# Retention and MLP on one core: copies and v scaling given to other engines, one more tile transposed by DMA, a new order

## The chip, the core and the metric

The kernel runs on one core of one Trainium2 chip. The metric is device time in microseconds (us), the median of several runs. The engines are called as in the profile: PE is TensorE, DVE is VectorE, ACT is ScalarE, POOL is GpSimd, SP is SyncE (it only issues DMAs here).

## The reference

A retention recurrence with 4 batches, 8 heads, 768 positions and 64 channels a head gives `y`. An MLP with a residual is then applied to each position's 512 channels:

```python
gamma = 1.0 - 2.0 ** (-5.0 - np.arange(H))
for t in range(S):
    state = gamma * state + einsum('bhd,bhe->bhde', k[:, :, t], v[:, :, t])
    y[:, :, t] = scale * einsum('bhd,bhde->bhe', q[:, :, t], state)
x = y.transpose(0, 2, 1, 3).reshape(B, S, H * D)
xn = (x - mean) / sqrt(var + 1e-6) * g_ln
out = x + maximum(xn @ w_ch1, 0) @ w_ch2      # 512 -> 2048 -> 512
```

Inputs and output are fp32.

## The kernel before

**Tiles.** The positions are cut into chunks of 128, six a batch. That makes 24 tiles of 128 positions with all heads. Tiles 0 to 3 are the first chunks of the four batches; then come the five later chunks of each batch in turn (tile 4 is batch 0's second chunk, tile 9 is batch 1's).

**The order is written out by hand.** `ORDER` is one list of tokens. Each token emits the instructions of one small step, and each engine takes its own instructions in just that order; waits on data are added by the framework. A token has a name, a tile or group number, an optional engine after the first slash (A for ACT, D for DVE, S for SP) and, after the second, the PSUM banks that it writes. There are eight banks: X0 to X3, Y0, Y1, M and PD. `warm` tokens are matmuls on zeros that compute nothing.

**One tile, step by step.** The tokens and their lines:

- `k`, `q`, `v` (L340): loads from HBM, cast to bf16, issued by POOL. Tile 0's q and k come by `hk`, `hq` (L348, fp32, from ACT and SP) and are cast by `hkc`, `hqc` (ACT or DVE, L243, L245). `gk`, `gq`, `gv` (L369) are one-element copies on POOL that touch a buffer that is to be loaded anew.
- Tiles below `T0` have q and k transposed on PE (`tk`, `tq`, L375). `ek` (L245) copies k out of PSUM, and `eq` (L389) multiplies q by the decay table `qsc` on DVE. Later tiles have both transposed by one DMA on SP's queue (`tr`, L383), and `eq` then reads from SBUF and multiplies by the fp32 table `arg`.
- `vis` (L398): the 128 x 128 scores of each head, into two X banks a tile; for tiles from `T0` on also q times the state (L404). From tile 8 on, a visit takes two tiles at once.
- `am` (L411): scores times the decay mask, DVE. `py` (L426): scores times v, PE; for tiles 4 to `T0 - 1` also q times the state (L420).
- `vg` (L455): v times the decay table `vsc`, for the state. One POOL instruction of 128 x 512.
- `pd` (L463): k times that v, added up in bank PD over a batch's chunks. `pb` (L473) makes the bf16 state of the next chunk from it, on DVE. A batch has one state chain; three `vg` and three state buffers are in use in turn.
- `bn`, `xn` (L434, L444): statistics and centred input of the MLP, DVE. `xc` (L450): a bf16 copy of y for the residual, ACT.
- `tx` and `ex` (L484, L245): transposes of `xn` on PE and a DVE copy out of PSUM for tiles below `TX` = 8. Later tiles take a DMA transpose on SP's queue (L493).
- `m` (L518): first MLP product, four blocks of 128 hidden channels for one tile (or a group of two or four tiles) into an X bank. `r` (L529 on ACT, L531 on DVE): relu out of that bank into `h1`.
- `z` (L541): second MLP product, in quarters of four blocks. `ad` (L548): scale by 1/std and add the residual, DVE. `st` (L555): store, from ACT's queue.
- `W`, `Z` (L359, L364): the two weights in four pieces each, cast to bf16, from POOL's queue.
- `sq`, `rs`, `sqt`, `gch`, `qsc`, `vsc`, `mask`, `zero`, `consts`, `idn`, `cm`, `lmul`, `arg`: tables, constants and standard deviations.

All DMAs share 16 DMA engines. [...]

## Time and profile before

| | |
|---|---|
| median of 3 runs | 214.94 us (214.89 to 215.52) |
| the profiled execution's own time | 215.48 us |
| its span in the profile | 213.7 us |
| PE busy | 205.1 us, 96% (`warm`: 10.5 us) |
| DVE, ACT, POOL busy | 135.1, 71.8, 97.9 us |
| `m` (L518) and `z` (L541) on PE, as listed | 93.7 us; 62.7 + 21.8 us and smaller groups |
| `vg` on POOL | 20 of 1091 ns |
| `eq` on DVE | 17 of 835 ns from `tr`, 7 of 416 to 424 ns from PSUM |
| `tr` on SP's queue | 17, median 7.4 us to landing |
| store to landing | 2.7 us |

The span runs from the first to the last instruction of one execution; 1.8 us of that execution's time lie around it. Busy time on PE counts matmuls whose ends are modelled. An engine's idle time matters only where PE waits for it.

### The profile page before, as it was taken

The page shows a single profiled execution, that of the slowest core. Times are in us where ns is not written, and L with a number is a line of the kernel's source. Part 1 is how long each engine was busy: PE and PEld are TensorE (multiplying, and loading weights), DVE is VectorE, ACT ScalarE, POOL GpSimd, SP SyncE. Part 2 cuts the span into 40 slices and gives each one's busy share as a digit, 9 for nine tenths or more (in the row PEclk, how much of TensorE's full clock was granted, in tenths as well). Part 3 has the DMA queues.
Part 4 walks back from the last instruction along what each step waited for, and adds up shares of the span by engine and source line. Part 5 has one row for each costly group of instructions (what it writes and reads, how often), then busy time and mean ns, then how long its engine had stood idle before and what let it go on. Part 6 is the DMA issues. An engine that isn't in the chain of part 4 may idle for free.

```text
span 213.7 us, 4986 instructions
## 1 busy us (share of the span) xinstructions
PE 205.1 (96%) x2035; PEld 132.1 (62%) x2035; DVE 135.1 (63%) x309; ACT 71.8 (34%) x157; POOL 97.9 (46%) x145
## 2 busy tenths in 40 slices
PE   7989989999999999979999999999999999999994
PEld 2558889887566657647678678565545444444443
DVE  6798899858739878699469357598787401030023
ACT  5133635342211511603505523423092620444400
POOL 8986585892796880886775279210000000000000
PEclk9999999999999999999999999999999999999999
DMA  9999999999999999999999999966132230121005
GB/s 127 175 180 180 166 192 169 204 151 148 114 120 193 74 175 121 145 205 148 137 136 181 150 121 176 165 99 198 25 75 26 59 95 0 49 98 49 33 19 196
DMA packets 109946, 27.11 MB, mean 127 GB/s; under 512 B 102625, under 2 KB 106977, under 8 KB 109922
## 3 DMA queue, kind: packets, MB, share of 16 engines
q0 software_dynamic: 77024, 13.37, 89.1%
q1 hardware_dynamic: 28242, 6.85, 25.1%
q10 hardware_dynamic: 4656, 6.56, 9.5%
q8 instruction: 16, 0.26, 0.5%
q14 instruction: 8, 0.07, 0.1%
HBM read 27.30 MB, written 6.29 MB: 157 GB/s over the span
## 4 chain that ended last, share of the span: by engine, by line
PE 72%; DMA 16%; POOL 6%; DVE 3%; issue 1%; POOLq 0%; DVEq 0%; SPq 0%
PE X L518 29%; PE M L541 24%; PE Y L541 9%; DMA tr<-qk 5%; DMA q<-in_q_dram 4%; DMA v<-in_v_dram 4%; PE PD L541 3%; DMA qk<-in_q_dram 3%; PE X L398 2%; DVE trq L389 2%; PE Y L426 2%; PE PD L463 2%; POOL v L340 1%; POOL q L340 1%; POOL k L340 1%
## 5 line engine op out<-in xcount | busy, mean ns | idle before, releaser
L518 PE MATMUL X<-xnt,w 128*128 128x128 bf16 (+2 forms) x896 | 93.7, 257 | 0.9 <-DVE xnt L245 0.6
L529 ACT ACTIVATE h<-X 128x512 bf16<-128x512 f32 x88 | 50.5, 600 | 105.8 <-PE X L518 97.9
L518 PEld LDWEIGHTS <-w 128*128 128x128 bf16 x896 | 66.6, 98 | 22.2 <-issue 1.1
L541 PE MATMUL M<-w,h 128*128 128x512 bf16 (+1 forms) x272 | 62.7, 370 | 0.0
L541 PEld LDWEIGHTS <-h 128*128 128x128 bf16 x400 | 37.3, 98 | 37.6
L411 DVE TENSOR_TENSOR asb<-X,mask 128x512 bf16<-128x512 f32 x48 | 30.4, 683 | 7.9 <-PE X L398 7.7
L455 POOL TENSOR_TENSOR vg<-v,vsc 128x512 bf16<-128x512 bf16 x20 | 21.7, 1091 | 8.9 <-DMA v<-in_v_dram 6.7
L340 POOL DMA_DIRECT2D v<-in_v_dram x24 | 21.8, 909 | 3.6 <-DMA w<-in_moe_w_ch_dram 2.0
L434 DVE BATCH_NORM_STATS2 bns<-Y 128x6 f32<-128x256 f32 (+1 forms) x40 | 17.0, 461 | 9.6 <-PE Y L426 9.4
L541 PE MATMUL Y<-w,h 128*128 128x512 bf16 (+1 forms) x96 | 21.8, 370 | 0.0
L450 ACT CAST x_all<-Y 128x256 bf16<-128x256 f32 (+1 forms) x40 | 15.1, 417 | 16.7 <-DVE xn L444 14.3
L444 DVE SCALAR_TENSOR_TENSOR xn<-Y,mv,gb 128x256 bf16<-128x256 f32 (+1 forms) x40 | 19.1, 515 | 0.5
L473 DVE TENSOR_TENSOR state<-PD,gch 64x256 bf16<-64x256 f32 x40 | 16.7, 416 | 3.6 <-PE PD L463 3.2
L548 DVE SCALAR_TENSOR_TENSOR osb<-M,rstd,x_all 128x512 f32<-128x512 f32 (+1 forms) x17 | 12.2, 720 | 7.9 <-PE M L541 7.7
L340 POOL DMA_DIRECT2D qk<-in_q_dram x17 | 15.1, 888 | 1.3 <-issue 1.1
L340 POOL DMA_DIRECT2D qk<-in_k_dram x17 | 15.3, 898 | 0.5 <-issue 0.4
L548 DVE SCALAR_TENSOR_TENSOR osb<-PD,rstd,x_all 128x512 f32<-128x512 f32 x2 | 1.5, 752 | 21.5 <-PE PD L541 21.5
L389 DVE TENSOR_TENSOR trq<-tr,arg 128x512 bf16<-128x512 bf16 x17 | 13.9, 835 | 1.4 <-DMA tr<-qk 1.3
L548 DVE SCALAR_TENSOR_TENSOR osb<-Y,rstd,x_all 128x512 f32<-128x512 f32 (+1 forms) x6 | 4.3, 727 | 15.8 <-issue 11.4
L369 POOL COPY scrap<-qk 1x1 bf16<-1x1 bf16 x28 | 5.3, 188 | 17.3 <-DMA qk<-in_q_dram 9.0
L562 PE MATMUL PD<-zeros 128*128 128x512 bf16 (+1 forms) x37 | 9.5, 392 | 1.2 <-DVE zeros L249 1.2
L426 PEld LDWEIGHTS <-asb 128*128 128x128 bf16 x192 | 7.7, 98 | 2.1 <-DVE asb L411 0.7
(74 smaller groups left out, 133.3 us busy)
## 6 DMA issues: line engine op xcount, KB each, us to landing
out_dram<-osb ACTq DMA_DIRECT2D x23, 256.0 KB, 2.7
w<-in_moe_w_ch_dram POOLq DMA_DIRECT2D x8, 512.0 KB, 9.6
v<-in_v_dram POOLq DMA_DIRECT2D x24, 128.0 KB, 6.4
qk<-in_k_dram POOLq DMA_DIRECT2D x17, 128.0 KB, 6.8
qk<-in_q_dram POOLq DMA_DIRECT2D x17, 128.0 KB, 6.3
k<-in_k_dram POOLq DMA_DIRECT2D x6, 128.0 KB, 8.3
q<-in_q_dram POOLq DMA_DIRECT2D x6, 128.0 KB, 7.6
tr<-qk SPq DMA_TRANSPOSE x17, 7.4
```

Of the source, the lines that this page charges most:

```text
L340: nc.gpsimd.dma_start(out=dst, in_=tok[kind][TILES[t]])
L389: nc.vector.tensor_tensor(out=slot(trq, t), in0=x, in1=qsc if t < T0 else arg, op=ALU.mult)
L411: nc.vector.tensor_tensor(out=slot(asb, t)[:, :, par, :], in0=bank(("pa", t, par)).rearrange("p (i t) -> p i t", t=P), in1=mask.rearrange( ...
L434: nc.vector.bn_stats(out=bns[:, t, i, :], in_=x)
L444: nc.vector.scalar_tensor_tensor(out=dst, in0=src, scalar=mv[:, t, 0:1], in1=g, op0=ALU.subtract, op1=ALU.mult)
L450: nc.scalar.copy(out=dst, in_=src)
L455: nc.gpsimd.tensor_tensor(out=slot(vgs, chunk(t)), in0=v_of(t), in1=vsc[:, c, :].unsqueeze(2).to_broadcast([P, H, D]), op=ALU.mult)
L473: nc.vector.tensor_tensor(out=slot(state, chunk(t) - 1)[o, :, o], in0=pd[o, :, o], in1=gch[o, c - 1, :].unsqueeze(2).to_broadcast([D, NPAI ...
L518: nc.tensor.matmul(bank(("mm", g, ho))[:, j * n * P:(j + 1) * n * P], lhsT=w1[:, ko, (ho + j) * P:(ho + j + 1) * P], rhs=x[:, x0:x0 + n, k ...
L529: nc.scalar.activation(out=dst, in_=src, func=AF.Relu)
L541: nc.tensor.matmul(bank(("m2", t, piece))[:, 0:hi - lo], lhsT=slot(h1, t // 4)[:, ho, t % 4 * P:(t % 4 + 1) * P], rhs=w2[:, ho, lo:hi], st ...
L548: nc.vector.scalar_tensor_tensor(out=slot(osb, t + piece)[:, 0:hi - lo], in0=bank(("m2", t, piece))[:, 0:hi - lo], scalar=rstd[:, t:t + 1] ...
```

## The change

Six things are changed:

- `T0` goes from 7 to 6, so tile 6's q and k are transposed by DMA, and the `k0` buffers go from 7 to 6.
- `ek` and `ex` (below `TX`) carry their engine in the token. Four of the six `ek` and four of the eight `ex` are on ACT, the others on DVE.
- `vg` can run on ACT, as eight activations (`Copy` with a scale from `vsc`), one a head. The five of tiles 0, 4, 5, 6 and 7 stay on POOL; fifteen go to ACT.
- `qscf`, which made the fp32 table in `arg`, is gone; `eq` multiplies by the bf16 table `qsc` in all tiles.
- The order is a new one throughout. `gch` and `sqt` come early, the state memsets (`zero`) and `consts` later; `hkc0` comes before `vsc`; `vg0` comes right after W0.
- The `warm` matmuls are 20 wide and 17 narrow ones instead of 23 and 14.

```diff
-CFG = {'T0': 7,
+CFG = {'T0': 6,
...
-           'k0': 7,
+           'k0': 6,
...
-hk0b/A hk0a/S iota small pos hq0b/A hq0a/S v0 grow table zero touch k1 idn lmul q1 consts arg
-vsc v1 hkc0/A qsc hqc0a/D W0 warm8_0 tk0//Y0 cm hqc0b/A k2 ek0 warm2_3 tq0//Y1 eq0 q2 mask
...
+hk0b/A hk0a/S iota small pos hq0b/A hq0a/S v0 grow table idn cm touch k1 arg lmul q1 hkc0/A vsc
+v1 hqc0a/D W0 warm8_1 tk0//Y0 hqc0b/A ek0/D qsc consts zero warm1_2 tq0//Y0 gch eq0 sqt vg0/
+mask warm2_3 vis0//X1,X3 gb//X2 k2 tk1//Y1 tq1//Y0 q2 am0a am0b ek1/A gl eq1 W1 warm2_3 py0//Y0
...
-    @on("qscf")
-    def _(eng):
-        nc.scalar.activation(out=arg, in_=arg, func=AF.Exp, bias=ln8, scale=1.0)
...
-        nc.vector.tensor_tensor(out=slot(trq, t), in0=x, in1=qsc if t < T0 else arg, op=ALU.mult)
+        nc.vector.tensor_tensor(out=slot(trq, t), in0=x, in1=qsc, op=ALU.mult)
...
+        if eng == "A":
+            for h in range(H):
+                nc.scalar.activation(out=slot(vgs, chunk(t))[:, h, :], in_=v_of(t)[:, h, :],
+                                     func=AF.Copy, scale=vsc[:, c, h:h + 1])
+            return
```

Three stretches of the new order, around the steps that the prediction speaks of:

```
Z1 r3_12/D ex4/D rs1 py5//Y1 Z2 m2_12//X1 bn5 tr6 m4_0//X0 m4_8//X3 pb6 xn5 ...
pd6 r4_4/A m5_12//X0 eq6 vg7/ Z3 pb7 vg1/A k9 vis6//X3,X2 m5_4//X1 am6a am6b ...
r7_4/A z4_2 vg11/A rs4 eq11 eq10 z4_3 ad4 rs7 tr13 sq6 vis10//X1,X2,X3,X0 tr12 pd11 ...
```

## The prediction

> **What bounds the kernel now.** I read the summary and the slices first: is one engine full throughout?

> ```profile
> span 213.7 us, 4986 instructions
> PE 205.1 (96%) x2035; PEld 132.1 (62%) x2035; DVE 135.1 (63%) x309; ACT 71.8 (34%) x157; POOL 97.9 (46%) x145
> ...
> DMA  9999999999999999999999999966132230121005
> ```

> TensorE (PE) is busy 96%, but part of that is `warm` filler (L562, 10.5 us), and the DMA rings are full for two thirds of the span. So I asked where PE stands still, by stretches (columns: stretch; length; busy us and instructions of each engine; granted clock; DMA share; GB/s):

> ```profile
> 16.00:49.00 33.00, 31.15 (x553) 28.48 (x552) 27.43 (x58) 14.31 (x33) 23.88 (x27) 1.00 1.90 176
> 49.00:66.00 17.00, 16.77 (x192) 10.93 (x184) 11.00 (x24) 3.51 (x7) 12.20 (x21) 1.00 2.08 131
> 66.00:94.00 28.00, 26.62 (x300) 17.96 (x293) 22.88 (x49) 8.75 (x22) 18.30 (x31) 1.00 1.60 147
> 94.00:211.00 117.00, 116.77 (x908) 67.61 (x906) 61.40 (x135) 39.66 (x86) 28.98 (x46) 1.00 0.83 104
> ```

> Idle on PE: 1.85, 0.23, 1.38 and 0.23 us. That is 3.7 us after 16 us: all that a better order can win there. The chain of waits in order of time says what holds it (start, length, piece):

> ```profile
> 37.35 10.51 DMA tr<-qk
> ...
> 89.88 3.04 DVE trq L389 x2
> ...
> 93.06 0.62 PE X L398 x16
> ...
> 210.81 0.35 DVE osb L548
> ```

> Tile 7's DMA transpose took 10.51 us; two `eq` took 3.04 us ahead of `vis12`. From the groups and timelines come the durations (count, busy us, mean ns):

> ```profile
> L455 POOL TENSOR_TENSOR vg<-v,vsc 128x512 bf16<-128x512 bf16 x20 | 21.7, 1091 | 8.9 <-DMA v<-in_v_dram 6.7
> ...
> L389 DVE TENSOR_TENSOR trq<-tr,arg 128x512 bf16<-128x512 bf16 x17 | 13.9, 835 | 1.4 <-DMA tr<-qk 1.3
> ...
> L245 DVE COPY trk<-Y 128x512 bf16<-128x512 bf16 x7 | 2.9, 418 | 0.1
> ...
> L506 ACT ACTIVATE rstd<-mv,epsb 128x1 f32<-128x1 f32 x8 | 2.0, 287 | 0.1
> ...
> L389 DVE TENSOR_TENSOR trq<-M,qsc 128x512 bf16<-128x512 bf16 x4 | 1.7, 416 | 0.0
> ...
> L313 ACT ACTIVATE gch<-lgq 128x4 f32<-128x4 f32 x5 | 0.6, 206 | 0.0
> ```

> and ScalarE's timeline (start, length) shows the table load finished before k0 is there:

> ```profile
> 1.88 1.28 ACT L292 ACT_TABLE_LOAD   x1 [1.88 <-issue]
> ...
> 4.15 0.62 ACT L243 CAST k<-osb 128x512 bf16<-128x512 f32 x1 [0.47 <-DMA osb<-in_k_dram]
> ```

> **My yardstick** is the lag L: the time of a point in PE's order minus the useful PE work ahead of it. Prices from the chain's own pieces: `m` 0.875 us, a `z` quarter 0.863, `vis` 0.28 a tile (0.40 with its state part), `py` 0.235 (0.455 with state), `pd` or four transposes 0.22, `gb` 1.1. Added along the order this is 192.3 us before. Before: L is 11.9 at `m0_0` (16.28 us), 14.7 at 21.3 us of work (36.03), 15.6 at `pd6` (44.39), 15.7 at `vis7` (48.66), 16.3 at `vis8`, 16.7 at `vis10`, 18.1 at `vis12` (93.06), 18.5 at the end (210.8).

> [...]
> - [...] most `eq` on tr take 0.69 us, but the two at 89.88 took 1.5 each while two `vg` ran on GpSimd (89.88 to 92.37).
> - [...] The trace has 0.416 with the bf16 table (PSUM source) and 0.69 with the fp32 table; from SBUF with bf16 it shows none.
> - [...] `gch` 206, `sq` with a pointer 287.
> - [...] tr landed in 9.7 to 10.5 us beside loads, 3.0 when loads were over (147.7).

> **The change part by part.**
> *Fifteen `vg` from GpSimd to ScalarE.* Each becomes eight 128x64 activations with a pointer scale. [...] The next: two `sq` in a row took 0.47, so 0.18 for one column[...]. [...] ScalarE gains 30 us in all, 72 to about 106 of 214; not the bound on average. But it is in order: behind a `vg` wait the `r` (L529) that free PE's X banks, `xc`, and the stores; if v is late, all of them. Three places are tight by the order: `vg11` begins about 58.2 us of work (after `r7_4` and copies), ends 60.2, `pd11` stands at 59.4; `vg2` 73.9 against 73.3; `vg15` 86.2 against 85.4. In full 2.2 us of PE wait. ScalarE's starts there rest on three copies placed by the order, not by their data, so I take 0.9. At 1.3 us none waits.
> On GpSimd 15 × 1.09 = 16 us go; its loads can issue earlier [...]: the 3.04 us before `vis12` becomes about 0.8, and its 1.28 us of PE idle goes. Next late there is tr12/tr13 (landed by 87.7); needed at 89.0.
> *The bf16 table.* `qscf` (0.72, ScalarE) goes[...]. Hidden by matmuls except in the place just counted: 0.
> *Copies.* Nine of 0.42 us leave VectorE (one with tile 6, eight to ScalarE at about 0.5). ScalarE is idle 18.7 of the 33 us there; 0 beyond the walk below.
> *Tile 6.* On PE 0.44 us of transposes go, and the state part costs 0.12 instead of 0.22: useful work 191.7, so -0.5. Added: one 256 KB transpose on SP's queue, in front of tr7, and a wait of `eq6` on it; behind `eq6` on VectorE stand `pb7` and both `am6`.
> *The start.* In the compiled order the table load is ScalarE's first computing instruction and stands behind the landing of SP's half of k0 (3.74 us): 3.74 + 1.28 = 5.02, k0's cast to 5.7, `tk0` 0.9 late. The state memsets (0.82) now stand before `eq0`: 7.5 instead of 6.86. Then `eq1`, `bn0`, `xn0` come before `am1`: `tx0` 12.9 (13.19 before), `m0_0` 14.9, `m0_4` 17.1 with 5.3 us done: L 11.8, as before: 0. `vg0` stands behind W0 on GpSimd and waits for v0 (6.58): k2 to k3 issue 1.8 late, but the rings still hold W0; I take 0.4 us for all later loads.
> *17 to 35 us, walked with these prices.* Waits after: 0.85 at `tq3` (q3 landed 20.0, now 20.4), 0.35 at `m2_4`, 0.4 elsewhere (`z1_0` on Z0, now held back by `vg4` until v4 is there). `m2_12` at 35.0, 21.3 us done: L 13.7 against 14.7: -1.0.
> *35 to 50 us.* Loads before q6 are as many bytes as before less one v: q6 lands about 35.1. tr6 beside v6, v7, Z1, Z2: nearest rows 10.5, 10.1, 9.7, and 5.9 at less load; I take 9.5: 44.6, `eq6` to 45.05. PE reaches `vis6` (28.7 us of work) at 43.1: waits 2.0. L 16.4 against 15.6: a lag of 0.8, which the lead above is already in. Bounds: tr6 in 7.4 (median of all), no wait, a lead of 1.2; in 10.5, a lag of 1.8. tr7 lands 3 us after tr6, before `vis7` at 50.9: 0.
> *After `vis7`.* Before L grew 2.8; now 0.6 to `vis12`, 0.9 for `vg`, 0.4 to the end: 1.9, so -0.9. The closing 2.9 us (last add and store) are as before.

> Sum: +0.8 - 0.9 - 0.5 = **-0.6 us**. The profiled execution took 215.48 (span 213.7 and 1.8 around it); the median of the runs is 0.54 under it, 214.94. So 214.9 for such an execution, **214.3** for the median. About 0.3%, 0.64 us, is what a measurement can tell from no change.

> **The rivals.**
> - *Slower: `vg` holds up ScalarE.* Place: `pd11`, `pd2`, `pd15`. For it: eight short instructions where there was one, in order, before relus. Against: ScalarE is half idle. The waits in full at 2.0 are 2.2 (+1.3 on the sum: 215.6), at 2.7 they are 4.3 (217.7); middle 216.6. It decides from waits of 2.1 us, a `vg` of about 2 us.
> - *Faster: the stages close up.* tr6 lands within 7.4: -2.0, 212.3; with `vg` at 1.3 too: 211.4. For it: the median landing; against: the three loaded ones.
> - *No change:* a bf16 table that speeds up nothing costs nothing either, and the stall before `vis12` may be tr13's; then +0.6: 214.9.

> **How the numbers follow.** My case (213.7 to 214.9) has 0.40, half of it under 214.3; the faster rival 0.25, the slower 0.35. So faster 0.45, same 0.20, slower 0.35. Range 211.6 to 217.2: the faster rival's ends, and the slower one's middle and a little more. My own case's range is 213.7 to 214.9.

> **What would show it.** Table load near 3.8 and `tk0` near 5.7; eight L454 activations in about 2.0 us; `eq` under 0.45 and never 1.5; PE waiting for tr6 before `vis6` near 43; no idle before `vis12`. If PE idles near `pd11`, `pd2`, `pd15` or before X writes by more than 2 us, the slower rival holds; with no wait at `vis6`, the faster one.

## The result and the profile after

The change makes the kernel slower. Four runs of it took 221.91 to 226.08 us, median **224.29**; the kernel before, on the same chip, 215.23. The ratio is **1.038** (95% interval 1.033 to 1.044). Here and below, medians are of all runs of a kernel, and ratios leave out those more than 1.5% above its fastest, such as the run of 226.08. The profiled execution took 221.91, against 215.48 before: 6.4 of the 9.1 us can be followed in the traces. The other three runs have no trace.

The summary, the granted clock and the DMA row of the kernel after:

```profile
span 219.9 us, 5073 instructions
...
PE 205.2 (93%) x2009; PEld 133.7 (61%) x2031; DVE 125.0 (57%) x302; ACT 103.1 (47%) x285; POOL 80.4 (37%) x130
...
PEclk9999999976999999999999999999999999999999
DMA  9999999999999999999999999973002030302213
```

The work has moved as the edit says: ScalarE from 71.8 to 103.1 us, GpSimd from 97.9 to 80.4, VectorE from 135.1 to 125.0. PE is as busy as before, in a longer span. New is the clock row: two slices (44 to 55 us) in which the granted clock is not full. The same stretches as before (stretch; length; busy us and instructions of PE, PEld, DVE, ACT, POOL; clock; DMA share; GB/s):

```profile
16.00:49.00 33.00, 27.65 (x479) 25.51 (x480) 22.45 (x46) 15.71 (x36) 23.17 (x27) 0.96 1.74 164
49.00:66.00 17.00, 16.84 (x172) 12.26 (x174) 10.45 (x25) 6.19 (x17) 7.19 (x14) 0.88 1.76 142
66.00:94.00 28.00, 27.43 (x304) 18.79 (x306) 20.37 (x52) 15.75 (x50) 16.95 (x33) 1.00 1.82 158
94.00:217.00 123.00, 120.22 (x944) 69.69 (x954) 60.53 (x139) 58.55 (x169) 18.84 (x37) 1.00 0.77 101
```

Idle on PE is 5.35 us in the first stretch (1.85 before), 0.57 in the third (1.38 before), 2.8 in the last (0.23 before). The second is full, but at clock 0.88: 172 instructions where there were 192. The groups that answer to those shown of before (count, busy us, mean ns):

```profile
L454 ACT ACTIVATE vg<-v,vsc 128x64 bf16<-128x64 bf16 x120 | 30.0, 338 | 0.9 <-ACT h L531 0.7
...
L386 DVE TENSOR_TENSOR trq<-tr,qsc 128x512 bf16<-128x512 bf16 x18 | 7.3, 413 | 4.7 <-DMA tr<-qk 4.7
L395 PE MATMUL X<-trq,tr 64*128 64x128 bf16 x144 | 6.0, 222 | 3.7 <-DVE trq L386 3.7
```

`eq` from `tr` fell from 835 to 413 ns, and PE waited 3.7 us in one place for one of them. The chain, in order of time, says which and why:

```profile
18.18 8.57 DMA v<-in_v_dram
...
26.83 1.04 POOL vg L457
27.87 0.76 POOL w L361
28.63 0.90 POOL qk L337
29.52 0.98 POOL vg L457
30.51 6.38 DMA qk<-in_q_dram
...
36.97 9.61 DMA tr<-qk
...
46.60 0.44 DVE trq L386
...
47.17 0.61 PE X L395 x8
47.78 0.21 PE Y L401 x8
47.99 1.82 PE X L520 x16
```

Read it from the top. v4 is issued at 18.18 and lands at 26.8. `vg4`, which waits for it, stands on GpSimd's queue ahead of the load of k6, and `vg5` ahead of q6. So q6 is issued at 30.51, lands at 36.9, its transpose lands 9.6 us later, and `vis6` starts at 47.17. The kernel before has `vg4`, k6, `vg5` and q6 in the same order on this queue; its lines for v4, `vg4` and q6:

```profile
16.12 0.88 POOL L340 DMA_DIRECT2D v<-in_v_dram  x1 [0.75 <-DMA w<-in_moe_w_ch_dram]
...
25.84 1.04 POOL L455 TENSOR_TENSOR vg<-v,vsc 128x512 bf16<-128x512 bf16 x1 [0.98 <-DMA v<-in_v_dram]
...
29.32 0.94 POOL L340 DMA_DIRECT2D q<-in_q_dram  x1
```

There v4 was issued 2.1 us sooner and landed 1.0 us sooner, and q6 landed at 35.7. It did no harm, since tile 6 then needed no DMA transpose.

In the last line of the chain 16 matmuls take 1.82 us, for which 0.875 is the price: they run at half pace. One step finer, PE's clock beside its idle time:

```profile
40.00:45.00 5.00, 3.48 (x63) 3.30 (x60) 1.10 (x2) 3.91 (x14) 5.00 (x6) 1.00 1.26 182
45.00:50.00 5.00, 2.83 (x36) 2.77 (x37) 2.46 (x5) 0.15 (x1) 3.66 (x5) 0.63 1.50 108
50.00:55.00 5.00, 4.95 (x52) 4.35 (x51) 3.37 (x8) 1.56 (x5) 0.12 (x1) 0.68 2.05 163
55.00:60.00 5.00, 4.95 (x80) 3.91 (x79) 3.31 (x9) 1.01 (x2) 1.13 (x6) 1.00 1.85 161
```

PE is idle from 43.5 to 47.2 (3.69 us); the clock is 0.50 from 46.3 to 53.2 us. It fell 2.9 us after PE had become idle, and it was full again after 6.0 us of work. The last section says what these times follow.

With the lag L (time less useful PE work ahead, as in the prediction), both profiled executions side by side:

| at | before | after | step before | step after |
|---|---|---|---|---|
| `vis5` | 14.5 | 14.2 | | |
| `vis6` | 15.5 | 18.5 | 1.0 | **4.3** |
| `vis7` | 15.7 | 21.4 | 0.2 | **2.9** |
| `vis12` | 18.1 | 22.4 | 2.4 | 1.0 |
| end of PE's work | 18.5 | 24.9 | 0.4 | **2.5** |

So +3.3 at `vis6`, +2.7 behind it, -1.4 to `vis12`, +2.1 to the end, -0.3 ahead of all this: +6.4, less 0.6 us of useful work. That is the 5.8 us by which PE's last work ends later (the addition behind it starts at 216.65, against 210.81). Another 0.4 us of the span lies behind that.

### The profile page after: what moved, and what is told of

The parts are those of the page before. It is cut to its first block, busy times and chain, and to the rows that moved or that the text cites. A ratio compares the mean times of both kernels' runs of the same rounds, so it can differ in the third digit from the quotient of the medians.

```text
span 219.9 us, 5073 instructions
## 1 busy us (share of the span) xinstructions
PE 205.2 (93%) x2009; PEld 133.7 (61%) x2031; DVE 125.0 (57%) x302; ACT 103.1 (47%) x285; POOL 80.4 (37%) x130
## 4 chain that ended last, share of the span: by engine, by line
PE 64%; DMA 20%; ACT 7%; DVE 3%; POOL 3%; issue 1%; ACTq 0%; DVEq 0%; SPq 0%
PE X L520 28%; PE M L543 20%; PE Y L543 8%; DMA tr<-qk 4%; DMA v<-in_v_dram 4%; DMA w<-in_moe_w_ch_dram 4%; DMA out_dram<-osb 4%; ACT vg L454 3%; DMA qk<-in_q_dram 3%; PE PD L543 3%; PE Y L423 2%; PE X L395 2%; ACT h L531 1%; POOL vg L457 1%; PE PD L465 1%
## 5 line engine op out<-in xcount | busy, mean ns | idle before, releaser
L531 ACT ACTIVATE h<-X 128x512 bf16<-128x512 f32 x88 | 50.9, 602 | 75.5 <-PE X L520 73.7
L520 PEld LDWEIGHTS <-w 128*128 128x128 bf16 x896 | 68.2, 100 | 22.0 <-DMA w<-in_moe_w_ch_dram 0.8
L543 PE MATMUL M<-w,h 128*128 128x512 bf16 (+1 forms) x271 | 64.4, 370 | 2.3 <-issue 0.6
L550 DVE SCALAR_TENSOR_TENSOR osb<-M,rstd,x_all 128x512 f32<-128x512 f32 (+1 forms) x18 | 13.0, 723 | 35.3 <-PE M L543 32.8
L454 ACT ACTIVATE vg<-v,vsc 128x64 bf16<-128x64 bf16 x120 | 30.0, 338 | 0.9 <-ACT h L531 0.7
L431 DVE BATCH_NORM_STATS2 bns<-Y 128x6 f32<-128x256 f32 (+1 forms) x41 | 16.9, 450 | 10.9 <-PE Y L423 10.8
L447 ACT CAST x_all<-Y 128x256 bf16<-128x256 f32 (+1 forms) x41 | 15.1, 402 | 15.7 <-DVE xn L441 15.5
L543 PE MATMUL Y<-w,h 128*128 128x512 bf16 x78 | 19.0, 379 | 0.1
L475 DVE TENSOR_TENSOR state<-PD,gch 64x256 bf16<-64x256 f32 x40 | 16.7, 416 | 3.9 <-PE PD L465 3.6
L337 POOL DMA_DIRECT2D qk<-in_q_dram x18 | 16.1, 893 | 1.2 <-DMA v<-in_v_dram 0.6
L386 DVE TENSOR_TENSOR trq<-tr,qsc 128x512 bf16<-128x512 bf16 x18 | 7.3, 413 | 4.7 <-DMA tr<-qk 4.7
L395 PE MATMUL X<-trq,tr 64*128 64x128 bf16 x144 | 6.0, 222 | 3.7 <-DVE trq L386 3.7
L564 PE MATMUL PD<-zeros 128*128 128x512 bf16 (+1 forms) x36 | 8.1, 362 | 1.4 <-DVE zeros L250 1.2
L395 PEld LDWEIGHTS <-tr 64*128 64x128 bf16 x144 | 4.2, 96 | 7.6 <-DMA tr<-qk 3.8
```

Of the source, the lines that this page charges most:

```text
L337: nc.gpsimd.dma_start(out=dst, in_=tok[kind][TILES[t]])
L395: nc.tensor.matmul(bank(("pa", t, par))[:, i * P:(i + 1) * P], lhsT=kT(t)[o, i, :], rhs=slot(trq, t)[o, i, :], start=True, stop=True)
L431: nc.vector.bn_stats(out=bns[:, t, i, :], in_=x)
L447: nc.scalar.copy(out=dst, in_=src)
L454: nc.scalar.activation(out=slot(vgs, chunk(t))[:, h, :], in_=v_of(t)[:, h, :], func=AF.Copy, scale=vsc[:, c, h:h + 1])
L475: nc.vector.tensor_tensor(out=slot(state, chunk(t) - 1)[o, :, o], in0=pd[o, :, o], in1=gch[o, c - 1, :].unsqueeze(2).to_broadcast([D, NPAI ...
```

## The experiments

Theory A: tile 6's transpose by DMA comes too late, PE waits, and its clock is halved. Rival B: ScalarE, full of `vg`, is what costs. Ratios are to the kernel before on the same chip: median 214.54 for e1 to e4, 215.16 for e5 to e8, 215.06 for e9, e10, b1 and b2, 214.55 for e11, b3 and b4, 215.28 for e12. Kernels of different chips are compared by their distance to it; the changed kernel lies 9.1 us above.

### Is it the wait for tile 6?

**e2_pe6**: tile 6 goes back to PE, all else stays.

```diff
-CFG = {'T0': 6,
+CFG = {'T0': 7,
...
-bn5 tr6 m4_0//X0 ... r0_12/D pd6 r4_4/A
+bn5 m4_0//X0 ... r0_12/D tk6//Y0 tq6//Y1 ek6/A pd6 r4_4/A
```

> The changed kernel with tile 6's q and k transposed on PE again (T0 = 7, tk6 and tq6 ahead of pd6), all else in the new order. Theory A: no wait for tr6 and no drop of the clock, 3.7 + 2.9 less, 0.5 more PE work: about 218.2 us. Rival B: no change beyond +0.5: 224 to 225.

Measured: 217.79, ratio 1.016 (1.008 to 1.023). L is 16.2 at `vis6` and 16.6 at `vis7`. As A says: the distance to the kernel before is 3.3 us and no longer 9.1. B expected no gain.

**e4_q6first**: tile 6 stays on the DMA, but its loads no longer stand behind `vg4` and `vg5`.

```diff
-eq4 vg4/ pb4 ... r2_8/A Z0 am4a ... am4b k6 ex3/A ... vg5/ q6 py4//Y0 ... z1_0//M Z1
+eq4 k6 q6 vg4/ pb4 ... r2_8/A am4a ... am4b ex3/A ... vg5/ Z0 py4//Y0 ... Z1
...
-m5_12//X0 eq6
+m5_12//X0 z1_0//M eq6
```

> The changed kernel with k6 and q6 issued ahead of vg4 and of Z0 on GpSimd's queue, Z0 after vg5, and z1_0, which needs Z0, moved behind m5_12 on PE. Theory A: q6 lands about 33.4 us instead of 36.9, tr6 about 43, when PE gets to vis6: no idle, no drop of the clock, about 6 us less, 218.3. If tr6 is still 2 us late, the clock's drop is shorter or gone: 220 to 222. Rival B: no change.

Measured: 217.55, ratio 1.014 (1.008 to 1.020); no wait for tile 6 (L 16.4, then 16.9). The distance is 3.0 us: the same gain by another way. What PE still waits for in this kernel (us in total, times, longest):

```profile
PE M L542 <- DVE osb L549: 1.3, 1, 1.3
...
PE PD L464 <- POOL vg L456: 0.9, 1, 0.9
PE X L519 <- DMA w<-in_moe_w_ch_dram: 0.8, 1, 0.8
PE Y L371 <- ACT k L243: 0.7, 1, 0.7
```

**e3_vgpool**: all `vg` on GpSimd again, the rest as changed.

```diff
-vg1/A ... vg9/A ... vg10/A ...
+vg1/ ... vg9/ ... vg10/ ...
```

> The changed kernel with all vg on GpSimd, as one instruction each, at the same places of the order. Rival B: most of the loss goes, 3 to 6 us less, 218 to 221. Theory A: the wait before vis6 and the clock's drop are still there (vis6 near 47, vis7 near 55.6); at most the 1.2 us by which the lag grew more after vis7 than before the change go[...]: 222.5 to 225.5.

Measured: 221.87, ratio 1.028 (1.017 to 1.039), between the two forecasts. The distance is 7.3 us, only 1.7 less than the changed kernel's, so B is not the main cause; e2 and e4, which leave the `vg` on ScalarE, say so more firmly. A was wrong on the clock: PE came to `vis6` late in this trace (46.1, after a slow start, see below), waited only 2.0 us, and its clock was not halved. A `vg` on GpSimd held it up 1.35 us at 107 us.

**b4_tr6**: the old order, with tile 6 on the DMA and the bf16 table, and nothing else of the change.

```diff
-CFG = {'T0': 7,
+CFG = {'T0': 6,
...
-m4_12//X1 bn5 ... tq6//Y0 rs5 tk6//Y1 r4_0/A eq6 ... ek6
+m4_12//X1 tr6 bn5 ... rs5 r4_0/A eq6 ...
```

> The kernel of b2 (old order, bf16 table) with tile 6's q and k transposed by DMA instead of by TensorE: tr6 stands ahead of bn5 on SP's queue, as in the changed kernel, and the loads of k6 and q6 stay where the old order has them. Theory A (the transpose needs its lead, whatever the order): q6 is issued at about 28 us there, lands at 34, the transpose takes 9.6 us and the multiplication 0.4, so that vis6 can start at 44.5 at the earliest; TensorE, with 0.7 us less to do, is there at 39.6: it stands idle 4 to 5 us, its clock is halved for about 6 us (mean granted clock 0.982 to 0.986), and the time is 213.9 - 0.6 + 4.5 - 1 + 2.9 = 219.7 us (218 to 221). Rival: the old order leaves the transpose enough time (the queue of loads on GpSimd is shorter there): no idle time over 2 us, no halved clock, 213.5 to 215.5 us.

Measured: 224.28, ratio 1.046 (1.038 to 1.054), 9.7 us above the kernel before and worse than expected. Its chain:

```profile
29.02 6.81 DMA qk<-in_q_dram
...
35.91 12.09 DMA tr<-qk
...
48.02 0.43 DVE trq L388
```

The transpose took 12.1 us to land here, not 9.6, and PE stood idle 8.7 us. So the wait comes with the transpose, in either order; the new order even shortens it.

### Is it the halved clock too?

**e1_fill** (the changed kernel) and **e6_tablefill** (e5, below) have 16 matmuls of zeros, 128x512 into X3, ahead of `vis6`: they compute nothing and only keep PE busy.

```diff
-k9 vis6//X3,X2
+k9 fill16//X3 vis6//X3,X2
```

> The changed kernel with 16 zero matmuls of 128x512 (3.5 us) into bank X3 ahead of vis6, in the 3.7 us in which PE stood idle for tr6; they compute nothing. Theory A (PE stands idle for tile 6's transpose, and its clock is halved after it): vis6 still starts near 47 us, but the clock stays full, and the 2.9 us by which the lag grew from vis6 to vis7 go: about 221.4 us against 224.3. Rival B (the eight-fold vg on ScalarE is what costs): no change, 224.3. Rival C (the clock's drop hides in waits on loads anyway): no change.

> The kernel of e5 with the 16 filling matmuls of zeros ahead of vis6. Theory A (the clock): the wait of 3.7 us for tile 6's transpose stays, since the matmuls only fill it, but the clock is not halved after it, so that the lag from vis6 to vis7 grows by 0.5 and not by 2.9 us: 221.0 - 2.4 = 218.6 us, granted clock 1.00 from 44 to 60 us. Rival B (the slow stretch after vis6 comes from the DMA traffic or from operands that come late, not from the idle time): the stretch stays slow, and the fill adds up to 0.5 us: 221.0 to 221.5 us.

Measured: e1 224.76, ratio 1.047 (1.040 to 1.054); e6 221.20, ratio 1.029 (1.021 to 1.036). In both, the clock stayed at 1.00 around `vis6`, and the lag grew by 0.5 (e1) and 1.4 us (e6) from `vis6` to `vis7` instead of 2.9. Of the two, e6 is the test: its other work was done at 43.6, and the fill lasted to 47.3, when tile 6 was there. In e1 the wait would have been 1.5 us only. The kernel of e6, same view as above:

```profile
45.00:50.00 5.00, 4.64 (x63) 3.10 (x62) 2.69 (x6) 0.82 (x2) 4.09 (x5) 1.00 1.51 104
50.00:55.00 5.00, 4.44 (x63) 3.00 (x61) 3.63 (x9) 1.42 (x4) 0.00 (x0) 1.00 1.97 167
```

In the second stretch, behind the wait, 63 instructions ran at full clock, where the kernel after managed 52. The operands are the same and the DMA traffic nearly so (167 GB/s, against 163), so it is the idle time that halved the clock there. The totals missed. e1's profiled execution lost 3.5 us ahead of `vis2`, and its fill (45.9 to 49.4) then held `vis6` up. Later PE waited 2.5 us for a buffer that a late store held (the chain is shown below, under e8), with the clock halved for 3.4 us behind it: from `vis14` to `vis16` L grew 4.4 us, against 0.7 in the kernel after. e6 came out 3.2 us under the median of all of e5's runs, where 2.4 were expected of the fill; but e5's ratio, from two runs, is 1.032 (1.019 to 1.046), from which e6's 1.029 can't be told. Between the two profiled executions (221.14 and 220.83) no gain shows either, since e6's was 1.0 us later at `vis5` and tile 6 came 1.7 us later. So the fill keeps the clock up, and what that is worth in the whole time is not shown.

The mean granted clock of every run says it for executions without a trace as well:

| kernel | runs | PE idle ahead of `vis6` in the trace | mean granted clock of its runs |
|---|---|---|---|
| after, e5, e9 | 12 | 3.2 to 4.3 us | 0.982 to 0.985, one 0.968 |
| b4_tr6 | 4 | 8.7 us | 0.974 to 0.977 |
| e6 (with fill) | 4 | none, filled | 0.998 to 1.000 |
| e1 (with fill) | 4 | none, filled | 1.000 twice, 0.992 twice (the wait at 116 us in the traced one) |
| e2, e4 (no wait) | 8 | none | 0.999 to 1.000 |

A clock of 0.984 over 220 us is 3.5 us of clock lost. The trace shows 2.4 us of it as lag (2.9 from `vis6` to `vis7` instead of 0.5); 0.4 fell into the end of the idle time.

### Is it the start?

**e5_table**: the table load early again.

```diff
-lmul q1 hkc0/A vsc v1
+lmul q1 vsc hkc0/A v1
```

> The changed kernel with one thing moved: the exponential vsc stands again ahead of the cast of tile 0's k on ScalarE's queue, as in the kernel before, so that ScalarE's table load runs while the DMA is on its way. Theory C (the start): the 0.8 us that TensorE stands idle at 4.9 us, for a cast that stands behind the table load, costs more than itself, because in most executions the matmuls of the first 14 to 17 us then run at half pace. So: tk0 at about 4.8 us with no idle time over 0.3, 0.40 us for its successors, the broadcast of g 1.1 us long and not 2.07, vis2 at about 15.5 us; 221.0 us (the profiled execution of the changed kernel, 221.9, less 0.8), 3 us under the changed kernel's median of 224.3, and the runs within 1.5 us of each other. Rival: the slow first 14 us of three of the profiles have another cause (the first matmuls' number, the DMAs); then the gain is at most the 0.8 us, 223.5 us, with runs as far apart as before.

Measured: 224.45 median (220.83 to 227.12), ratio 1.032 (1.019 to 1.046), an interval that says little. PE's first steps of this kernel, and then those of e3, which has the late table load:

```profile
1.59 3.30 PE L563 MATMUL PD<-zeros 128*128 128x512 bf16 x8
4.69 0.63 PE L371 MATMUL Y<-idn,k 128*128 128x128 bf16 x4
```

```profile
5.69 0.61 PE L371 MATMUL Y<-idn,k 128*128 128x128 bf16 x4 [0.80 <-ACT k L243]
...
6.82 0.58 PE L371 MATMUL Y<-idn,q 128*128 128x128 bf16 x4
```

The idle 0.8 us is gone, but `vis2` came at 16.07 (16.24 in the kernel after), and neither median nor spread moved: theory C's forecast fell. What stays is an observation: of six profiled executions with the late table load, three (e1, e2, e3) ran their matmuls at half pace until 14 to 17 us and reached `vis2` 2.6 to 3.7 us late; of the seven with the early one, none did (e7's lost 1.1 us later, at a half clock from 10.9 to 14.3 us). The clock row is full in e1, e2 and e3 all the same, but only because it counts time without a record as full: their clock records begin at 16.8, 13.9 and 17.2 us, those of the other traces at 4.0 to 7.0. Right there the matmuls go from half to full pace (wide ones on zeros from 0.43 to 0.22 us apart). So the slow start looks like half clock as well, and the mean clock (1.000 in e2 and e3) does not show it.

**e9_again**: the changed kernel unaltered, for a second trace.

> The changed kernel once more, for a second profiled execution, because the first (221.9 us) was the fastest of its four and the others, up to 226, have no trace. Theory C (slow start in most executions): a profile of 224 us or more has vis2 at 18.5 to 20 us and not at 16.2, and from vis5 on the same steps. Theory E (longer landings): vis2 at about 16.2, but the transpose of tile 6 lands later, 12 us and not 9.6, and TensorE stands idle over 5 us ahead of vis6. In both the clock is halved for about 6 us after the idle time, and the mean granted clock of every run is 0.982 to 0.986.

Measured: 223.92 (222.12 to 230.33), ratio 1.039 (1.032 to 1.046), profiled at 222.12. It had no slow start (`vis2` at 16.08); the transpose took 9.8 us, PE stood idle 4.3 us, and the clock was 0.982. The profiled execution was again the fastest of its four, so neither theory on the slower runs was put to the test.

### What is left once the wait is gone?

**e7_tableq6** is e4 with e5's edit. **e8_stores** is e7 with two stores put earlier on ScalarE's queue:

```diff
-st2/A r8_14/A ... st5/A r9_8/A ... r9_2/A st3/A vis14//X1,X0,X2,X3 st4/A vg16/A
+st2/A st3/A r8_14/A ... st5/A st4/A r9_8/A ... r9_2/A vis14//X1,X0,X2,X3 vg16/A
```

> The kernel of e4 (k and q of tile 6 loaded ahead of vg4) with the early table load of e5. If the two costs add up: e4's median 217.55 less 0.8 us of idle time, and less again if e4's runs had the slow start in part: 216.5 us (215.8 to 217.0); no idle time ahead of vis6, clock 1.00 at 44 to 60 us, lag at vis6 about 15.6 and at vis8 about 16.3, as in the kernel before. Left over are then about 1.5 us, from the stores and the scalings on ScalarE's queue at 100 to 125 us. Rival: the early start is eaten by the next wait (the landing of W1 or of tile 2's k and q), then 217.5.

> The kernel of e7 with two stores (tiles 3 and 4) put on ScalarE's queue earlier, beside those of tiles 2 and 5, instead of behind the scalings of v of tiles 14 to 16. Theory D: the wait of tile 9's result for a buffer whose store was issued late (1.26 us of TensorE in e4 at 113 us) goes: e7 less 1.2 us, 215.3 us, lag at vis16 about 18.5. Rival: the buffer that is waited for is another's, or the relus that are behind become the wait; then it is e7's time within 0.4 us.

Measured: e7 218.10, ratio 1.010 (1.006 to 1.015); e8 217.19, ratio 1.009 (1.006 to 1.013). e7 is no better than e4: the rival's 217.5 is the nearer one. In e8's trace no wait for an `osb` buffer is left; it had cost 0.3 us in e7's, 1.3 in e4's. But by the ratios e8 is only 0.2 us under e7, as the rival said, and not the 1.2 of theory D. In the kernel after, this chain had built up at 107 to 117 us:

```profile
106.94 1.90 ACT vg L454 x8
...
109.59 0.43 ACT x_all L447 x2
110.02 6.08 DMA out_dram<-osb
...
116.19 0.76 DVE osb L550
...
117.00 1.02 PE M L543 x4
```

A store stands behind a `vg` and copies on ScalarE's queue and lands late; VectorE waits for its buffer, PE for VectorE: 0.5 us here, 1.0 to 2.5 us in the traces of e1, e2, e4, e5, e6 and e9.

**e11_v6first**: e8 with v6 loaded ahead of v7, and `vg21`, `vg22` on GpSimd.

```diff
-r3_0/A v7 vis5//X3,X1 ... xc4 v6 tx4//Y0
+r3_0/A v6 vis5//X3,X1 ... xc4 v7 tx4//Y0
```

> The kernel of e8 (new order, tile 6's loads and the table load early, two stores early) with v of tile 6 loaded ahead of v of tile 7, and v of tiles 21 and 22 scaled by GpSimd again. Theory: two waits go that e8's trace shows, 1.2 us at 42.6 us (the state's product of tile 6 waits for vg6, which waits for v6's landing) and 0.5 us at 148.3 us (h behind vg22 on ScalarE): 217.2 - 1.5 = 215.7 us. Rival: vis6 then waits for the transpose that the 1.2 us hid: only the 0.5 us, 216.7.

Measured: 218.77 (217.41 to 220.76), ratio 1.023 (1.012 to 1.033). Neither theory. The two waits went (`vis6` at 43.07, L 14.4), and tile 7's transpose took them back. Its chain:

```profile
31.46 7.09 DMA qk<-in_q_dram
...
38.56 11.54 DMA tr<-qk
...
50.47 0.49 DVE xn L440
...
51.01 0.40 PE Y L485 x4
```

`eq7` waits for that transpose and holds half of `xn6` up behind it on VectorE; PE stood idle 3.1 us there, at a clock that stayed full.

**e10_allpool**: e8 with e3's edit.

> The kernel of e8 with all scalings of v on GpSimd again (1.05 us each instead of 2.0 on ScalarE). Theory B1: ScalarE's relus and stores are no longer behind the scalings; the waits on h (0.5 us at about 150 us) and on vg (0.5 us) go, and GpSimd, which also gates k, q and v, brings some back (1.35 us at 107 us in the kernel of e3): 216.2 to 217.2 us, no more than 0.8 us from e8's 217.2. Rival: GpSimd becomes the bound for the gates of the middle (80 to 130 us): 218.5 us or more.

Measured: 219.90, ratio 1.021 (1.015 to 1.027): 2.7 us worse than e8, the rival. PE waited 4.6 us for `vg` in three places. In the new order GpSimd cannot take the `vg` back.

**e12_pe6fix**: e2 with the repairs of e5, e8 and e11 (its `vg21`, `vg22`).

> The kernel of e2 (new order, tile 6's q and k transposed by TensorE) with the repairs of e5, e8 and e11: table load early, stores of tiles 3 and 4 early, v of tiles 21 and 22 scaled by GpSimd. Theory F (the transpose of tile 6 by DMA is all that is wrong with the change): no wait over 1 us is left anywhere, clock 1.00, lag 11.3 at vis2, 15.7 at vis8, 17.5 at vis14 and vis22: 214.3 us (213.5 to 215). Rival (the new order and the scalings on ScalarE cost something by themselves, spread over waits of 0.3 to 0.5 us): 215.5 to 217 us.

Measured: 215.48, ratio **1.001** (0.999 to 1.004), just under the rival's range and over theory F's. L is 16.2 at `vis8`, 17.8 at `vis14`, 18.2 at `vis22`, and the clock row is full. So with tile 6 on PE and three small repairs the rest of the change costs nothing that can be measured, and brings nothing. The repairs together take the distance from e2's 3.3 us to 0.2; which of them does it is not separated.

### Each part alone, in the old order

**b1_vg_act**: the fifteen `vg` on ScalarE, by the eight activations of the change.

```diff
-vg1 ... vg9 ... vg10 ...
+vg1/A ... vg9/A ... vg10/A ...
```

> The kernel before, in its own order, with one part of the change alone: v is scaled for the states by ScalarE, eight multiplications by a column each, for the same 15 tiles. Theory B1 (from the traces of the changed kernel: 8 in 2.00 us, relus and stores behind them late by up to 2.5 us in the stretch 100 to 155 us): it costs 1 to 2 us, 215.7 to 217 us, with TensorE waiting for h behind vg or for osb behind a store. Rival: GpSimd's queue was what held up the gates and so the transposes, and relieving it of 15 scalings (1.1 us each) gains about as much as ScalarE's loss: within 0.6 us of the kernel before.

Measured: 217.80, ratio 1.012 (1.005 to 1.018): 2.7 us slower, more than expected. Three waits of PE carry the loss (in brackets the idle time and its releaser):

```profile
105.15 0.81 PE L545 MATMUL M<-w,h 128*128 128x512 bf16 x3 [1.44 <-DVE osb L552]
...
134.49 1.03 PE L522 MATMUL X<-xnt,w 128*128 128x256 bf16 x8 [1.31 <-ACT h L533]
...
140.06 0.62 PE L397 MATMUL X<-trq,tr 64*128 64x128 bf16 x16 [0.86 <-ACT h L533]
```

The 2.7 us are net. With no `vg` on GpSimd beside them, the two `eq` ahead of `vis12` took 1.29 us and not 3.03, and the stall there was gone: L at `vis12` is 16.3, against 18.1 before. In this trace PE gained 1.8 us by then and lost 4.5 afterwards.

**b2_bf16**: the bf16 table alone.

```diff
-pd0 qscf q4
+pd0 q4
...
-in1=qsc if t < T0 else arg
+in1=qsc
```

> The kernel before, in its own order, with another part of the change alone: VectorE multiplies the DMA-transposed q by the bf16 table, and the exponential of the f32 table is left out. Theory: the multiplication takes 0.41 and not 0.84 us, and the stall before vis12 (lag 16.3 at vis8 to 18.1 at vis12; 16.9 to 17.5 in the kernel of e8) shrinks to 0.6 us: 1.2 us less, 213.8 us. Rival: the stall is one of DMA landings (the transposes of tiles 12 and 13), for which the multiplication comes 0.4 us sooner only: 0.4 us less; or nothing, within 0.3.

Measured: **213.89**, ratio **0.9955** (0.993 to 0.998): as expected, and the one version that beats both kernels. VectorE at the place in question, in the kernel before and then in this one:

```profile
89.88 3.03 DVE L389 TENSOR_TENSOR trq<-tr,arg 128x512 bf16<-128x512 bf16 x2
```

```profile
89.51 1.01 DVE L388 TENSOR_TENSOR trq<-tr,qsc 128x512 bf16<-128x512 bf16 x2
```

L grows 0.3 us from `vis8` to `vis12`, not 1.8: the stall was the multiplication's, and not a landing's. b1 and b2 together say that it needed both, the fp32 table and a `vg` on GpSimd: in these traces either part of the change ends it alone, so the gain comes once.

**b3_copies**: b2 with the copies of k and x split between ScalarE and VectorE as in the change.

```diff
-ek1 ... ex1 ... ek3 ... ek4 ... ex3 ... ek5 ... ex6 ... ex7
+ek1/A ... ex1/A ... ek3/A ... ek4/A ... ex3/A ... ek5/A ... ex6/A ... ex7/A
```

> The kernel of b2 (old order, bf16 table) with the copies of the transposed k of tiles 1, 3, 4, 5 and x of tiles 1, 3, 6, 7 by ScalarE instead of VectorE, as the changed kernel has them. Theory (the prediction's own reading: they are beside other work): within 0.5 us of b2, 213.4 to 214.4 us. Rival: on ScalarE they stand behind relus, and the matmuls that read them start later: 214.5 to 216 us.

Measured: 214.69, ratio 0.9995 (0.997 to 1.002): above the theory's range and in the rival's. By the ratios that is 0.9 us over b2, just clear of the noise. The rival's way is not what the trace shows: the copies did bring PE forward (L 13.3 at `vis6`, against 14.8 in b2), but `vis7` then waited 1.9 us for tile 7's transpose, and the clock dropped to half for 3.4 us: by `vis8` the lead had become a lag (17.6, against 16.1 in b2). Of the 19 runs in its ratio, seven have a mean clock of 0.991 or 0.992 and average 215.5 us; the other twelve average 214.1.

## Why the prediction was wrong

Predicted were 214.3 us and -0.6; it came to 224.3. Step by step, on the profiled execution:

- **The start and the walk to `vis6`: right within 0.4 us.** Table load at 3.75, `tk0` at 5.72, `tx0` 12.99 (12.9), `m0_0` 14.99 (14.9). L at `vis5` is 14.2, 0.3 less than before, and PE was ready for `vis6` at 43.5 (43.1).
- **tr6's wait (2.0 us, L 16.4): the term that was mis-sized first.** The transpose was right, 9.6 us against 9.5. Wrong was q6's landing, 36.9 and not 35.1. I had it follow from bytes in the rings, "as many bytes as before less one v", and from 0.4 us for all later loads. The chain shows that q6 is issued when GpSimd's queue gets to it, behind `vg4`, which waits for v4; that held before the change too. In the new order `vg0` stands ahead of k2, and the loads from there on were issued 0.9 to 2.1 us later than before. v4 landed 1.0 us later, and q6 was issued 1.2 us later; a v less in the rings brought nothing to a load that was not yet issued. (In e9 q6 was issued as early as before, at 29.26, and landed at 36.4.) I had seen `vg4` hold back Z0 and `z1_0`, and not the loads behind it. PE idled 3.7 us, and L became 18.5: 2.1 us more. My bound of a transpose in 10.5 us reached to a lag of 1.8 over before; measured are 3.0. e4 takes just these loads out from behind the `vg`, and the wait is gone.
- **What follows the wait: a term that the sum did not have.** I priced an idle time at its length. From `vis6` to `vis7` L grew 2.9 where I had taken what it was before, 0.2. e6 and the clocks of all runs show that the idle time halved the clock, for 6.0 us of work here.
- **After `vis7` (1.9 us, a gain of 0.9): measured 3.5, a loss of 0.7.** To `vis12` 1.0 (0.6 predicted), so the stall's end was right and is worth 1.2 us by itself (b2); b1 shows the `vg` on GpSimd in it, as I had it, and b2 that the table alone ends it. From there on 2.5 (1.3 predicted). A `vg` on ScalarE took 2.0 us (eight activations in 2.02 at 106.81). My 2.0, with 1.3 and 2.7 as its bounds, was an estimate that the traces of before do not show; it held, the places were wrong. `pd` waited only 0.25 us twice; what suffered was what stands behind a `vg` on ScalarE's queue, relus and stores, which I had named and given no price. b1 puts this part at 2.7 us net in the old order.
- **The rivals.** The slower one named `vg` on ScalarE; its own places, where `pd` waits, cost 0.5 us. That a wait at `vis6` could decide was in the text, but only as a bound of my own case, with no case beyond it.
- **The useful work, 191.7 us: right. The copies, put at 0:** one took 0.58 to 0.59 us on ScalarE in the kernel after (I had about 0.5) and 0.42 on VectorE; in the old order they cost 0.9 us (b3), since PE's lead is lost again, and more, at tile 7's transpose. What they cost in the changed kernel is not shown.

Errors of the sum: 2.1 + 2.7 + 1.6 = 6.4, to -0.6: +5.8, what PE's end shows.

**Open**: the other 2.6 us between the medians. The untraced runs of the changed kernel, of e5 and of e9 took 223 to 227 us and one 230; e6, with the fill, stayed at 223.0 or under. The three traces of that wait show 3.2, 3.7 and 4.3 us, so a longer wait in those runs is possible, a slow start as well, which their mean clocks would not show; neither was seen.

## What to carry to other kernels

Price an idle time on TensorE at its length and at the half-clock stretch that may follow it: 3.7 us of waiting cost 6 us of lag here. A wait of 1.9 us did it too in b3, and one of 3.1 us in e11 was spared. Walk the queue that issues a load before dating its landing, with every computing step in it that waits for data of its own. Try the parts of a change alone: here one line gains 0.45%, and tile 6's transpose, in the old order, costs 5% (b4 over b2).
